# Cross-covariance attention and a gated feed-forward on one core: q and k loads queued 24 slots ahead, half of the batch-end products spread over the slots, and table loads placed ahead of PSUM copies

## The chip, the cores and the metric

The kernel runs on 1 core of one Trainium2 chip. The metric is device time in microseconds (us); 3 runs of the kernel before gave a median of 888.96 us (887.82 to 889.47). The engines are named as in the profile: PE is TensorE, DVE VectorE, ACT ScalarE, POOL GpSimd, and SP the engine that issues stores and transposes.

## The reference

For each of 4 batches, q, k and v are 6016 x 256. The columns of q and k are divided by their norms over the 6016 rows, a 256 x 256 score is made, a softmax is taken over its last axis, and v is multiplied by it. All 24064 rows then go through a gated feed-forward with 1536 hidden columns.

```python
qn = q / (np.linalg.norm(q, axis=1, keepdims=True) + 1e-06)
kn = k / (np.linalg.norm(k, axis=1, keepdims=True) + 1e-06)
s = kn.transpose(0, 2, 1) @ qn / tau
a = softmax(s)                      # over the last axis
x = (v @ a).reshape(B * S, D)
gate = 1.0 / (1.0 + np.exp(-(x @ w_gate)))
out = (gate * (x @ w_val)) @ w_out
```

## The kernel before

**The tiling.** A batch's 6016 rows are 47 tiles of 128 rows, in 12 chunks of 4 tiles (the last chunk has 3). The attention matrix is folded into the feed-forward's weights: G = a w_gate and H = a w_val (`gh`, 12 parts for each batch), so a chunk of v, transposed (`vT`), needs only two products: gate = vT G and val = vT H. The 1536 hidden columns are 12 slices of 128; one slice of one chunk is a *slot*, so a batch has 144 slots, and the main loop runs over b, ci (chunk) and f (slot).

**A slot.** `glu` (L460) puts two matmuls for `ps_gate` and two for `ps_val` on PE, a sigmoid on ACT (L481, to `g_sb`) and a multiplication on DVE (L482, to `hT`). `ps_gate` and `ps_val` have two buffers each, so PE can run two slots ahead of ACT and DVE. `a_sum` (L488, L499) makes sums of slices of `hT` on DVE, five for each half of a chunk: those of the first half in the chunk's own slots 6 to 10, those of the second half in slots 0 to 4 of the next chunk.

**The output products.** The product with w_out works on pairs of row tiles with seven products instead of eight, from such sums. A chunk of 4 tiles has 2 pairs, each of 42 matmuls into two PSUM banks (`ps_o`, 2 buffers): 84 in `out_work` (L530), done while the next chunk is in its slots. `run_work(work, share)` (L592) issues a share of what is left, normally 1 / (12 - f), so 7 products in each slot. When a bank is full, `evict` is put on a list; `flush` (L602) runs it: a copy on ACT from PSUM to `m_sb` (L564) and, after the second bank, `combine` (L515, five operations on POOL). `store` (L607) issues the chunk's output from SP at slot 4.

**The next batch's score.** During a batch, the score of the next one is made beside it. `side_work` (L703) hands out its steps by slot: `load_qk` (L124, two DMAs issued by POOL for a group of 4 tiles), `score` (matmuls into `ps_s`), squares on ACT and their accumulation on DVE, over slots 0 to 95. In batches 1 and 2 group g has its first score product in slot 8g, and its load 20 slots earlier, but not before slot 0: groups 0 to 2 are thus loaded in slot 0 itself, and the load of group 3 in slot 4 follows them on POOL. `qkpool` has 5 buffers for each of q and k. In batch 0 the loads stand 12 slots ahead. Each chunk also has a v load, for the chunk two further on, at its slot 0 (POOL, L139), and a transpose by DMA, for the next chunk, at its slot 2 (SP, L446).

**The batch end.** In chunks 9 and 10 of batches 0 to 2 (`block`) the slots hold no output products. All 84 stand in a block after slot 11, in four quarters; ahead of each quarter come the side steps of that place, and `flush` behind it. In chunk 9's block stand `wide_sqrt` (ACT) and two `wide_inv` (DVE); in chunk 10's `wide_scale` (DVE) and two `exps` (ACT). Square root, exponential and sigmoid need different tables on ACT: a table load stands where the function changes. Copies need none. The parts of G and H for the next batch are made in chunk 11.

**The end.** The last chunk's own output cannot lie beside another chunk: `end_rows` and `last_rows` multiply its 3 tiles plainly after its slots.

Of the kernel before, what the change touches and what calls it, by code (L numbers as in the profile page):

```python
# [11 lines left out]
ACT = mybir.ActivationFunctionType  # L12
# [33 lines left out]
def kernel(  # L46
# [20 lines left out]
    nc = tc.nc  # L67
# [5 lines left out]
    B, N, C = q.shape  # L73
# [4 lines left out]
    FC = DFF // P  # L78
    FG = 512
    NFG = DFF // FG  # L80
    TPC = 4
    CH = TPC * P
    NCH = (NT + TPC - 1) // TPC
    groups = [(t, min(TPC, NT - t)) for t in range(0, NT, TPC)]
# [58 lines left out]
    t0, nt = groups0[0]  # L143
# [289 lines left out]
    def gh(b, n, pl, tag, act=None):  # L433
        gh_store(b, n, gh_mms(b, n, pl, tag), n % 2 == 0 if act is None else act)
# [4 lines left out]
    def transpose_v(b, ci, ps=None, late=None):  # L439

        t0, nt = groups[ci]
        v_sb = vs.pop((b, ci))
        vT = vtpool.tile([P, TPC * CB, P], BF16, tag="vT", name="vT")
        flat = v_sb[:, :nt, :].rearrange("p t c -> p (t c)")
        if ps is None:
            nc.sync.dma_start_transpose(out=vT[:, : nt * CB, :], in_=flat)  # L446
        else:
            for n in range(nt * CB):
                nc.tensor.transpose(
                    out=ps[:, n, :], in_=flat[:, ds(n * P, P)], identity=ident_bf  # L450
                )
            half = nt * CB // 2 if late else nt * CB
            if late:
                late(vT[:, half : nt * CB, :], ps[:, half : nt * CB, :])
            nc.vector.tensor_copy(out=vT[:, :half, :], in_=ps[:, :half, :])
        vts[b, ci] = vT.rearrange("p (u cb) n -> p cb u n", cb=CB)
# [3 lines left out]
    def glu(b, ci, f, between=None):  # L460
        t0, nt = groups[ci]
        n = nt * P
        G, H = st[b]["gh"]
        vT = vts[b, ci]
        if f == 0:
            hts[b, ci] = hpool.tile([P, FC, CH], BF16, tag="hT", name="hT")
        ps_gate = psg.tile([P, CH], FP32, tag="g", name="ps_gate")
        ps_val = psv.tile([P, CH], FP32, tag="v", name="ps_val")
        for ps, w in ((ps_gate, G), (ps_val, H)):
            for ib in range(CB):  # L470
                mm(
                    ps[:, :n],
                    w[f // (FG // P)][:, ib, ds(f % (FG // P) * P, P)],
                    vT[:, ib, :nt, :],
                    start=(ib == 0),
                    stop=(ib == CB - 1),
                )
            if between is not None and w is G:
                between()
        g_sb = gpool.tile([P, CH], FP32, tag="g", name="g_sb")  # L480
        nc.scalar.activation(out=g_sb[:, :n], in_=ps_gate[:, :n], func=ACT.Sigmoid)  # L481
        nc.vector.tensor_tensor(  # L482
            out=hts[b, ci][:, f, :n], in0=ps_val[:, :n], in1=g_sb[:, :n], op=ALU.mult
        )
# [3 lines left out]
    def a_sum(b, ci, g, m):  # L488

        nt = groups[ci][1]  # L490
        half = nt // 2
        hT = hts[b, ci]
        if m == 0:
            sums[b, ci, g] = spool.tile(
                [P, len(A_SUMS), FC // 4, CH // 2], BF16, tag=f"s{g}", name="sums", bufs=2 - g
            )
        (r0, k0), op, (r1, k1) = A_SUMS[m]
        f0, f1 = g * (FC // 2), (g + 1) * (FC // 2)
        nc.vector.tensor_tensor(  # L499
            out=sums[b, ci, g][:, m, :, : half * P],  # L500
            in0=hT[:, f0 + k0 : f1 : 2, ds(r0 * half * P, half * P)],
            in1=hT[:, f0 + k1 : f1 : 2, ds(r1 * half * P, half * P)],
            op=op,
        )
# [84 lines left out]
                work.append((2, single, state, nt - 1, f))  # L589
        return work  # L590

    def run_work(work, share):  # L592

        left = sum(w[0] for w in work)
        upto = left * share
        done = 0
        while work and done < upto:
            cost, fn, *args = work.pop(0)
            fn(*args)
            done += cost  # L600

    def flush():  # L602
        while pending:
            fn, *args = pending.pop(0)
            fn(*args)

    def store():  # L607
        while stores:
            b, ci = stores.pop(0)
            t0, nt = groups[ci]  # L610
            nc.sync.dma_start(out=out_rows[b][:, t0 : t0 + nt, :], in_=ffn.pop((b, ci))[:, :nt, :])
# [37 lines left out]
    for g, (t0, nt) in enumerate(groups0):  # L649
# [6 lines left out]
        while adds:  # L656
            w, last_sq = adds.pop()
# [45 lines left out]
    def side_work(b):  # L703


        side = {}

        def at(slot, fn, *a):
            side.setdefault(divmod(slot, FC), []).append((fn, a))

        for ci in range(NCH):
            nb, nci = (b, ci + 1) if ci + 1 < NCH else (b + 1, 0)
            lb, lci = (b, ci + 2) if ci + 2 < NCH else (b + 1, ci + 2 - NCH)
            if (nb, nci) == (0, 1):
                at(8, lambda: transpose_v(0, 1, psm.tile([P, TPC * CB, P], BF16, tag="m", name="ps_tp")))
            elif nb < B:
                at(ci * FC + 2, transpose_v, nb, nci)
            if lb < B:
                at(ci * FC + 0, load_v, lb, lci)
            if (b, ci) == (0, 0):  # L720
                for i in range(FC // TPC):
                    at(i, load_w_out, i)
                    at(i + 2, sum_w_out, i)
        n = b + 1
        if n == B:
            return side
        first, last = (14 if b == 0 else 0), 8 * FC
        for g, (t0, nt) in enumerate(groups):
            s0 = first + g * (last - first) // NCH
            at(max(0, s0 - (12 if b == 0 else 20)), load_qk, n, t0, nt)  # L730
            for u in range(nt):
                at(first + (t0 + u) * (last - first) // NT, score, n, t0, u)
            if g == 0:
                at(s0, acc_start, n)
            for i, (fn, w) in enumerate(((acc_square, 0), (acc_add, 0), (acc_square, 1), (acc_add, 1))):
                at(s0 + 1 + 2 * i, fn, n, g, w)
        for i in range(6):
            at(8 * FC + 2 + i, acc_fold, n, *divmod(i, 3))
        at(9 * FC + 9, norms_mm, n)
        for ci, s, *call in (  # L740
            (9, 0, wide_sqrt, n),
            (9, 2, wide_inv, n, 0),
            (9, 3, wide_inv, n, 1),
            (10, 0, wide_scale, n),
            (10, 0, exps, n, 0),
            (10, 0, exps, n, 1),
        ):
            side.setdefault((ci, FC + s), []).append((call[0], call[1:]))
        at(11 * FC + 0, sums_both, n)
        at(11 * FC + 0, gh_tiles, n)  # L750
        for i in range(len(gh_order)):
            at(11 * FC + min(i + 1, FC - 1), gh, n, i, *((pss, "s"), (psm, "m"))[i % 2])
        return side
# [5 lines left out]
    prev = None  # L759
    for b in range(B):  # L760
        side = side_work(b)
        for ci in range(NCH):
            block = b + 1 < B and ci in (9, 10)
            for f in range(FC):
                first = (b, ci, f) == (0, 0, 0)
                glu(b, ci, f, (lambda: gh(0, 4, pso, "o", act=False)) if first else None)
                flush()
                if prev is not None:
                    if f == 4:
                        store()  # L770
                    if not block:
                        run_work(work, 1 / (FC - f))
                    if f < len(A_SUMS):
                        a_sum(*prev, 1, f)
                if f >= FC // 2 and f - FC // 2 < len(A_SUMS) and (b, ci) != (B - 1, NCH - 1):
                    a_sum(b, ci, 0, f - FC // 2)
                for fn, a in side.get((ci, f), ()):
                    fn(*a)
                if (b, ci) == (0, 0):
                    for i in gh_first.get(f, ()):  # L780
                        gh(0, i, pso, "o")
            if prev is not None and block:
                for s in range(TPC):
                    for fn, a in side.get((ci, FC + s), ()):
                        fn(*a)
                    run_work(work, 1 / (TPC - s))
                    flush()
            prev = (b, ci)
            if prev != (B - 1, NCH - 1):
                work = out_work(*prev)  # L790
# [40 lines left out]
```

## Time and profile before

| what | value |
|---|---|
| median of 3 runs | 888.96 us |
| the profiled execution | 889.01 us, of which the span from first to last instruction is 887.2 us |
| busy PE / DVE / ACT / POOL | 812.7 / 739.6 / 533.0 / 422.1 us |
| mean granted PE clock | 0.982 |
| DMA | 78.23 MB moved, 88 GB/s on average |

The busy times overlap, and the one nearest to the span is the candidate for what sets the end. A timeline row gives start, length, engine, line, operation, what is written and read, and in brackets how long the engine had been idle before and what ended the wait. Line 119 is the helper through which all matmuls go, so matmuls are told apart by their tiles. Rows of busy time by stage give the stage, its length, then busy time with the instruction count for PE, PE's weight loads, DVE, ACT and POOL, then the granted clock, the DMA engines' share and GB/s. A matmul's length is longer than the distance from one to the next, since they are pipelined; for throughput one takes the distance between starts.

### The profile page before, as it was taken

To read this page: it belongs to the slowest core of one execution; us is meant where nothing else is said; L and a number is where in the kernel's file an instruction comes from. 1 tells how busy PE (TensorE), PEld (TensorE's weight loads), DVE (VectorE), ACT (ScalarE), POOL (GpSimd) and SP (SyncE) were. 2 spreads that over 40 slices of the span, in tenths; PEclk is the share of its full clock that TensorE was granted. 3 is DMA by queue.
4 is the path that set the end of the run, shared out by engine and by line. 5 is a ranking of instruction groups with operands and counts; after the bars stand their busy time and mean duration, and the time that the engine had idled before them with its cause. 6 is when DMAs were issued, how large, how long until landed. Compare 5 with 4: busy or idle time off the path is not lost.

```text
span 887.2 us, 17830 instructions
## 1 busy us (share of the span) xinstructions
PE 812.7 (92%) x6772; PEld 501.3 (57%) x6772; DVE 739.6 (83%) x1236; ACT 533.0 (60%) x900; POOL 422.1 (48%) x623
## 2 busy tenths in 40 slices
PE   4899999999849999999984999999998999999997
PEld 2546666654525666665553566666555666666665
DVE  5698999998646999999864699999986898888885
ACT  3657666656635666665663566666566655555553
POOL 3655464534342465553434246555343345555554
PEclk9999999999988999999998899999999999999999
DMA  9975557322245565632234556563223223232311
GB/s 221 214 143 100 100 98 138 71 49 68 58 79 100 104 106 96 121 66 48 64 62 73 102 107 107 96 117 69 48 62 65 57 47 86 58 85 60 75 41 66
DMA packets 77926, 78.23 MB, mean 88 GB/s; under 512 B 50704, under 2 KB 55824, under 8 KB 77840
## 3 DMA queue, kind: packets, MB, share of 16 engines
q0 software_dynamic: 21216, 38.02, 25.9%
q1 hardware_dynamic: 56336, 38.48, 18.6%
q8 instruction: 53, 0.87, 0.4%
q10 hardware_dynamic: 288, 0.59, 0.2%
q14 instruction: 33, 0.27, 0.1%
HBM read 78.64 MB, written 24.64 MB: 116 GB/s over the span
## 4 chain that ended last, share of the span: by engine, by line
PE 71%; DVE 12%; DMA 6%; ACT 5%; issue 5%; POOL 1%; DVEq 0%; ACTq 0%; POOLq 0%
PE ps_gate L119 23%; PE ps_o L119 22%; PE ps_val L119 21%; DVE sums L499 6%; DVE hT L482 5%; DMA k_sb<-in_k_dram 5%; PE ps_s L119 3%; ACT g_sb L481 2%; PE ps_gh L119 2%; ACT sq L231 2%; DMA w_gate<-in_moe_w_gate_dram 1%; ACT m_sb L564 0%; ACT L304 0%; DVE acc L269 0%; DVE two L279 0%
## 5 line engine op out<-in xcount | busy, mean ns | idle before, releaser
L481 ACT ACTIVATE g_sb<-ps_gate 128x512 f32<-128x512 f32 (+1 forms) x576 | 338.3, 589 | 294.9 <-PE ps_gate L119 287.1
L482 DVE TENSOR_TENSOR hT<-ps_val,g_sb 128x512 bf16<-128x512 f32 (+1 forms) x576 | 387.0, 673 | 120.4 <-ACT g_sb L481 83.5
L119 PE MATMUL ps_val<-vT,gh_H 128*128 128x512 bf16 (+1 forms) x1152 | 339.2, 376 | 7.3 <-DVE hT L482 5.2
L119 PE MATMUL ps_gate<-vT,gh_G 128*128 128x512 bf16 (+1 forms) x1152 | 339.3, 376 | 2.2 <-ACT g_sb L481 2.2
L499 DVE TENSOR_TENSOR sums<-hT 128x768 bf16<-128x768 bf16 (+1 forms) x470 | 303.3, 645 | 0.0
L522 POOL TENSOR_TENSOR m_sb<-m_sb 128x256 f32<-128x256 f32 x91 | 65.8, 723 | 422.4 <-ACT m_sb L564 422.4
L119 PEld LDWEIGHTS <-sums 128*128 128x128 bf16 x2730 | 184.7, 98 | 98.7 <-DVE sums L499 21.3
L119 PEld LDWEIGHTS <-gh_H 128*128 128x128 bf16 x1152 | 112.9, 98 | 148.3 <-issue 24.5
L119 PE MATMUL ps_o<-w_sums,sums 128*128 128x128 bf16 x1638 | 152.5, 220 | 1.2 <-DVE sums L499 0.9
L119 PE MATMUL ps_o<-w_out_sb,sums 128*128 128x128 bf16 x1092 | 108.1, 219 | 12.2 <-DVE sums L499 12.2
L119 PEld LDWEIGHTS <-gh_G 128*128 128x128 bf16 x1152 | 99.6, 98 | 32.3 <-issue 3.1
L525 POOL TENSOR_TENSOR out_sb<-m_sb 128x128 f32<-128x128 f32 x182 | 112.6, 638 | 0.0
L119 PE MATMUL ps_s<-k_sb,q_sb 128*128 128x256 bf16 x376 | 73.4, 301 | 40.9 <-DMA k_sb<-in_k_dram 34.3
L119 PEld LDWEIGHTS <-hT 128*128 128x128 bf16 x1176 | 82.9, 98 | 47.4 <-issue 6.2
L564 ACT COPY m_sb<-ps_o 128x512 f32<-128x512 f32 (+1 forms) x182 | 95.6, 527 | 9.7 <-PE ps_o L119 9.6
L119 PE MATMUL ps_o<-w_sums,hT 128*128 128x128 bf16 x1092 | 90.1, 220 | 4.7 <-ACT m_sb L564 4.2
L523 POOL TENSOR_TENSOR m_sb<-m_sb 128x256 f32<-128x256 f32 x91 | 80.2, 881 | 7.1
L528 POOL TENSOR_TENSOR out_sb<-m_sb 128x256 f32<-128x256 f32 x91 | 78.5, 863 | 0.0
L119 PEld LDWEIGHTS <-q_sb 128*128 128x128 bf16 x376 | 34.3, 107 | 47.6 <-issue 36.5
L231 ACT ACTIVATE sq<-k_sb 128x1024 bf16<-128x1024 bf16 (+2 forms) x44 | 44.8, 1026 | 15.1 <-DMA k_sb<-in_k_dram 14.9
L269 DVE TENSOR_TENSOR acc<-acc,sq 128x1024 bf16<-128x1024 bf16 (+1 forms) x66 | 50.5, 766 | 0.0
L231 ACT ACTIVATE sq<-q_sb 128x1024 bf16<-128x1024 bf16 (+2 forms) x36 | 36.5, 1015 | 0.2 <-DVE acc L660 0.2
(79 smaller groups left out, 280.4 us busy)
## 6 DMA issues: line engine op xcount, KB each, us to landing
out_dram<-out_sb SPq DMA_DIRECT2D x44, 512.0 KB, 3.4
v_sb<-in_v_dram POOLq DMA_DIRECT2D x44, 256.0 KB, 5.2
q_sb<-in_q_dram POOLq DMA_DIRECT2D x35, 256.0 KB, 7.0
k_sb<-in_k_dram POOLq DMA_DIRECT2D x35, 256.0 KB, 7.8
q_sb<-in_q_dram POOLq DMA_DIRECT2D x4, 512.0 KB, 12.4
k_sb<-in_k_dram POOLq DMA_DIRECT2D x4, 512.0 KB, 14.8
w_f<-in_moe_w_out_dram SPq DMA_DIRECT2D x3, 512.0 KB, 15.4
out_dram<-out_sb SPq DMA_DIRECT2D x3, 384.0 KB, 6.7
```

Source lines behind the costliest of these rows:

```text
L119: nc.tensor.matmul(out, lhsT=lhsT, rhs=rhs, start=start, stop=stop, **kw)
L231: nc.scalar.activation(out=sq[:, :nt, :], in_=src[:, :nt, :], func=ACT.Square)
L269: nc.vector.tensor_tensor(out=acc[:, :nt, :], in0=acc[:, :nt, :], in1=st[b]["sq", w][:, :nt, :], op=ALU.add)
L481: nc.scalar.activation(out=g_sb[:, :n], in_=ps_gate[:, :n], func=ACT.Sigmoid)
L482: nc.vector.tensor_tensor(out=hts[b, ci][:, f, :n], in0=ps_val[:, :n], in1=g_sb[:, :n], op=ALU.mult)
L499: nc.vector.tensor_tensor(out=sums[b, ci, g][:, m, :, : half * P], in0=hT[:, f0 + k0 : f1 : 2, ds(r0 * half * P, half * P)], in1=hT[:, f0 ...
L522: nc.gpsimd.tensor_tensor(out=t, in0=t, in1=m[:, 3:4, :].to_broadcast([P, 2, P]), op=ALU.add)
L523: nc.gpsimd.tensor_tensor(out=t, in0=t, in1=m[:, 4:6, :], op=ALU.subtract)
L525: nc.gpsimd.tensor_tensor(out=blocks[:, mids, :], in0=m[:, 1 - n, :], in1=m[:, 4 + n, :], op=ALU.add)
L528: nc.gpsimd.tensor_tensor(out=ends, in0=t, in1=m[:, 0:2, :], op=ALU.add)
L564: nc.scalar.copy(m[:, n0:n1, :], state[bank][:, : (n1 - n0) * P].rearrange("p (n c) -> p n c", c=P))
```

## The change

Four things change, all of them places in the order; no instruction is added or dropped except that the table loads on ACT are asked for by name.

- *Loads.* In batches 1 and 2, group g is loaded 24 slots ahead of slot 8g. For groups 0 to 2 that place lies in the batch before, in slots 120, 128 and 136 (chunk 10, slots 0 and 8, and chunk 11, slot 4).
- *Products.* `run_work` takes `keep`, a number of products to leave. In chunks 9 and 10 the first pair's 42 products go into slots 0 to 10 and only the second pair's stand in the block, in two halves.
- *Tables.* In the blocks the load of the sigmoid's table is placed right behind the square root, and right behind the exponentials, and that of the exponential's table ahead of `wide_scale`. `flush` runs once before and once behind the block, so the copies come after the table loads.
- *The last chunk.* In the last chunk of the last batch the products of the chunk before are spread over 10 slots instead of 12, and `a_sum` stands ahead of `run_work` in all slots.

```diff
-    def run_work(work, share):
-
-        left = sum(w[0] for w in work)
-        upto = left * share
+    def run_work(work, share, keep=0):
+
+        upto = sum(w[0] for w in work[: len(work) - keep]) * share
         done = 0
-        while work and done < upto:
+        while len(work) > keep and done < upto:
...
-            at(max(0, s0 - (12 if b == 0 else 20)), load_qk, n, t0, nt)
+            if b == 0:
+                at(max(0, s0 - 12), load_qk, n, t0, nt)
+            elif s0 >= 24:
+                at(s0 - 24, load_qk, n, t0, nt)
...
+        if n + 1 < B:
+            for g, (t0, nt) in enumerate(groups[:3]):
+                at(NCH * FC - 24 + 8 * g, load_qk, n + 1, t0, nt)
...
+        table = nc.scalar.preload_act_table
         for ci, s, *call in (
             (9, 0, wide_sqrt, n),
-            (9, 2, wide_inv, n, 0),
-            (9, 3, wide_inv, n, 1),
+            (9, 0, table, ACT.Sigmoid),
+            (9, 1, wide_inv, n, 0),
+            (9, 2, wide_inv, n, 1),
+            (10, 0, table, ACT.Exp),
             (10, 0, wide_scale, n),
             (10, 0, exps, n, 0),
             (10, 0, exps, n, 1),
+            (10, 0, table, ACT.Sigmoid),
         ):
...
+            early = 1 if block else 2 if (b, ci) == (B - 1, NCH - 1) else 0
...
-                    if not block:
-                        run_work(work, 1 / (FC - f))
                     if f < len(A_SUMS):
                         a_sum(*prev, 1, f)
+                    held = len(work) if not block or f == 0 else held
+                    run_work(work, 1 / max(1, FC - early - f), held // 2 if block else 0)
...
             if prev is not None and block:
-                for s in range(TPC):
+                flush()
+                for s in range(3):
                     for fn, a in side.get((ci, FC + s), ()):
                         fn(*a)
-                    run_work(work, 1 / (TPC - s))
-                    flush()
+                    run_work(work, 1 / (2 - s) if s < 2 else 1)
+                flush()
```

How the change stands on ACT, in chunk 9 of batch 0 and its block. `g_sb` is a sigmoid, `m_sb` a copy of a bank, `n_sb` the square root. Before, from the chunk's second slot on:

```order
137 L481 ACTIVATE g_sb<-ps_gate 128x512 x11
138 L304 ACT_TABLE_LOAD
139 L304 ACTIVATE n_sb<-ps_n 128x258
140 L564 COPY m_sb<-ps_o 128x512
141 L564 COPY m_sb<-ps_o 128x384
142 L564 COPY m_sb<-ps_o 128x512
143 L564 COPY m_sb<-ps_o 128x384
144 L481 ACT_TABLE_LOAD
145 L481 ACTIVATE g_sb<-ps_gate 128x512 x12
```

The same place in the changed kernel:

```order
137 L481 ACTIVATE g_sb<-ps_gate 128x512 x6
138 L564 COPY m_sb<-ps_o 128x512
139 L481 ACTIVATE g_sb<-ps_gate 128x512 x5
140 L564 COPY m_sb<-ps_o 128x384
141 L304 ACT_TABLE_LOAD
142 L304 ACTIVATE n_sb<-ps_n 128x258
143 L796 ACT_TABLE_LOAD
144 L564 COPY m_sb<-ps_o 128x512
145 L564 COPY m_sb<-ps_o 128x384
146 L481 ACTIVATE g_sb<-ps_gate 128x512 x7
```

One copy of the first pair now lies among the sigmoids and one right behind the last of them; the sigmoid's table is loaded behind the square root, ahead of the two copies that are left, and no longer at the first sigmoid.

On POOL, from the v load in slot 0 of chunk 10 of batch 0 on, before (L139 loads v, L129 loads q or k, L522 to L528 are one `combine`):

```order
146 L139 DMA v_sb<-in_v_dram 128x1024
147 L522 TENSOR_TENSOR m_sb<-m_sb 128x2x128
148 L523 TENSOR_TENSOR m_sb<-m_sb 128x2x128
149 L525 TENSOR_TENSOR out_sb<-m_sb 128x128 x2
150 L528 TENSOR_TENSOR out_sb<-m_sb 128x2x128
```

In the changed kernel:

```order
146 L139 DMA v_sb<-in_v_dram 128x1024
147 L129 DMA q_sb<-in_q_dram 128x1024
148 L129 DMA k_sb<-in_k_dram 128x1024
149 L129 DMA q_sb<-in_q_dram 128x1024
150 L129 DMA k_sb<-in_k_dram 128x1024
151 L522 TENSOR_TENSOR m_sb<-m_sb 128x2x128
152 L523 TENSOR_TENSOR m_sb<-m_sb 128x2x128
153 L525 TENSOR_TENSOR out_sb<-m_sb 128x128 x2
```

The q and k loads of groups 0 and 1 of batch 2's score now stand between the v load and the next `combine`, two groups one behind the other.

## Prediction

> **What bounds the kernel now.** First the page's busy shares, then who TensorE (PE) waited for, then busy time by stage, then the timeline at the places that stood out.
>
> ```profile
> PE 812.7 (92%) x6772; PEld 501.3 (57%) x6772; DVE 739.6 (83%) x1236; ACT 533.0 (60%) x900; POOL 422.1 (48%) x623
> PE ps_s L119 <- DMA k_sb<-in_k_dram: 34.3, 7, 12.5
> ```
>
> PE is the busiest engine and VectorE (DVE) the next. Of PE's waits one stands out: the score product `ps_s` waits for a load of k, 34.3 us in 7 waits, the longest 12.5 us. The stages show where (each row: stage, its length, then busy time of PE, weight loads, DVE, ACT, POOL, then the granted clock, DMA share, GB/s):
>
> ```profile
> 254.10:266.58 12.48, 0.01 (x1) 0.03 (x1) 1.26 (x2) 0.24 (x1) 7.71 (x14) 0.65 0.66 126
> 266.58:271.60 5.02, 5.02 (x22) 2.66 (x23) 1.23 (x3) 2.14 (x3) 0.00 (x0) 0.50 1.13 205
> 271.60:283.40 11.80, 11.80 (x87) 7.19 (x85) 9.31 (x17) 7.89 (x13) 3.48 (x5) 1.00 0.25 47
> 270.00:436.00 166.00, 161.31 (x1356) 100.13 (x1355) 153.41 (x250) 107.51 (x181) 78.23 (x112) 1.00 0.47 87
> 488.95 0.58 PE L119 MATMUL ps_s<-k_sb,q_sb 128*128 128x256 bf16 x2 [12.34 <-DMA k_sb<-in_k_dram]
> ```
>
> In the first slot of batch 1 PE stands for 12.48 us, then works 5.02 us at half the clock, and is full again from 271.60. Batch 2 begins the same way (12.34 us before 488.95). Everywhere else in a batch PE is busy 97% of the time at clock 1.00 (161.31 of 166.00), so it sets the pace and DVE (92%) is close behind. The other holes lie at the end of each of batches 0 to 2, in chunks 9 and 10, where a chunk's 12 slots are followed by a block of products:
>
> ```profile
> 197.18:209.20 12.02, 11.49 (x57) 4.94 (x55) 11.83 (x23) 7.09 (x13) 4.37 (x6) 1.00 0.33 75
> 209.20:214.12 4.92, 4.86 (x86) 4.73 (x84) 4.43 (x7) 3.56 (x6) 1.72 (x3) 1.00 0.04 9
> 214.12:227.24 13.12, 11.78 (x52) 4.63 (x50) 10.50 (x20) 8.67 (x14) 4.99 (x9) 1.00 0.37 81
> 227.24:233.47 6.23, 4.84 (x85) 4.72 (x84) 2.43 (x5) 3.78 (x7) 1.84 (x4) 1.00 0.01 3
> 233.47:252.75 19.28, 18.46 (x164) 11.80 (x162) 14.40 (x29) 11.98 (x23) 7.95 (x14) 1.00 0.25 55
> ```
>
> Rows one and three are the slots of chunks 9 and 10, two and four their blocks, five is chunk 11. In the slots of chunk 9 DVE is busy 11.83 of 12.02 us: it, not PE, sets the pace there.
>
> **Part one, the loads.** In batches 1 and 2 the q and k loads of groups 0 to 3 all stand in the first slots:
>
> ```profile
> 257.39 0.57 POOL L139 DMA_DIRECT2D v_sb<-in_v_dram  x1
> 258.48 0.55 POOL L129 DMA_DIRECT2D k_sb<-in_k_dram  x1
> k_sb<-in_k_dram POOLq DMA_DIRECT2D x4, 256.0 KB, 7.6
> ```
>
> The first k load is issued at 258.48 and its user runs at 266.58, 8 us later; the last row, of the stage from 300 to 345 us, gives 7.6 us to landing. The change issues group 0 at slot 120 of the batch before, in chunk 10, some 30 us ahead of its use by the stage rows (13.12 + 6.23 + 19.28 less what the queue is late), so landing is covered several times over. What is late next is nothing on PE: from 271.60 it never waits. Gain for batch 1: 12.48 of standing plus half of 5.02, since that work at clock 1.00 takes 2.51, so 15.0. For batch 2: 12.34, and 2.3 for a slow stretch a little shorter, so 14.6. Together 29.6.
>
> The rule on the slow stretch differs a little: the Trainium skill (TensorE: Matmul & The Clock Gate, Part 1: The HAM clock gate) has the array back at full rate after about 3.4 us of sustained work; that would make each slow stretch cost 1.7 and the term 28.2. Here the row shows 5.02 us at 0.50.
>
> POOL issues the same number of loads, each of about 0.55 us as above, so its own time does not grow. The moved ones pass `combine` of chunks 9 and 10 in POOL's order, and stand behind the v load of chunk 10. There lies a cost: the transpose that makes `vT` of chunk 11 then runs beside four q and k loads.
>
> ```profile
> 218.62 0.57 POOL L139 DMA_DIRECT2D v_sb<-in_v_dram  x1
> 223.78 1.24 SPq L446 DMA_TRANSPOSE vT<-v_sb  x1
> vT<-v_sb SPq DMA_TRANSPOSE x3, 4.4
> vT<-v_sb SPq DMA_TRANSPOSE x1, 12.3
> ```
>
> It is issued 5.2 us after the v load. It took 4.4 us to land beside two loads (300 to 345 us) and 12.3 beside eight (256 to 268 us). Beside four I take 7, nearer to the first. Issued near 223.5 as now, it lands at 230.5. By the walk below, chunk 11's first gate must be done near 232.0, so `vT` must be there by 231.3: no cost, and 4.5 us each in batches 0 and 1 if 12.3 held.
>
> By the Trainium skill (DMA: Bandwidth & Descriptors, Queues, rings and completion order) each DMA engine takes turns between its queues packet by packet, so a transpose would never wait for all that is queued on POOL's; by that the loss is nothing. The row of 12.3 speaks against it, so I keep the loss as a rival.
>
> **Part two, the products of one pair.** A slot of `glu` alone takes PE 0.86 us, and 84 products in a row 4.92, so 0.0585 each and 2.46 for the 42 that move:
>
> ```profile
> 198.04 0.59 PE L119 MATMUL ps_gate<-vT,gh_G 128*128 128x512 bf16 x2
> 198.90 0.59 PE L119 MATMUL ps_gate<-vT,gh_G 128*128 128x512 bf16 x2
> ```
>
> Twelve slots are 10.32. Chunk 9's slots last 12.02; I leave 0.3 of the rest to the six short matmuls of `norms_mm`, so PE has 1.4 free and the last sigmoid comes 1.06 later. Chunk 10's last 13.12 with 2.8 free: the products fit, DVE sets the pace as before.
>
> **Part three, the order on ACT.** Chunk 9's block, before:
>
> ```profile
> 208.95 0.60 ACT L481 ACTIVATE g_sb<-ps_gate 128x512 f32<-128x512 f32 x1 [0.27 <-PE ps_gate L119]
> 209.57 1.28 ACT L304 ACT_TABLE_LOAD   x1
> 210.86 0.39 ACT L304 ACTIVATE n_sb<-ps_n 128x258 f32<-128x258 f32 x1
> 214.81 1.28 ACT L481 ACT_TABLE_LOAD   x1
> 216.11 1.09 ACT L481 ACTIVATE g_sb<-ps_gate 128x512 f32<-128x512 f32 x2
> 213.16 0.95 DVE L310 RECIPROCAL n_sb<-n_sb 128x128 f32<-128x128 f32 x1
> 216.74 0.69 DVE L482 TENSOR_TENSOR hT<-ps_val,g_sb 128x512 bf16<-128x512 f32 x1 [2.62 <-ACT g_sb L481]
> 232.72 0.59 ACT L564 COPY m_sb<-ps_o 128x512 f32<-128x512 f32 x1 [1.26 <-PE ps_o L119]
> 233.67 0.48 ACT L564 COPY m_sb<-ps_o 128x384 f32<-128x384 f32 x1 [0.36 <-PE ps_o L119]
> ```
>
> From the sigmoid's end (209.55) to the next sigmoid pass 6.56 us: table load, square root, four copies that wait for the products, table load. The change leaves one late copy 0.48, load 1.28, root 0.39, load 1.28, and two copies 0.59 + 0.48 (lengths from chunk 10's rows): 4.50. With the start at 210.61, the next sigmoid begins at 215.1 and DVE's `hT` 0.63 after it as now, at 215.7 instead of 216.74. DVE's inversion (root's end to 214.11, 2.86) ends at 215.6, so it does not come later. Gain 1.0, and DVE carries it through chunk 10. Its block:
>
> ```profile
> 226.80 0.60 ACT L481 ACTIVATE g_sb<-ps_gate 128x512 f32<-128x512 f32 x1 [0.41 <-PE ps_gate L119]
> 229.70 0.91 ACT L378 ACTIVATE e_sb<-x_sb,shift 128x256 bf16<-128x256 f32 x2 [1.01 <-DVE x_sb L320]
> 234.17 1.28 ACT L481 ACT_TABLE_LOAD   x1
> 235.46 0.87 ACT L481 ACTIVATE g_sb<-ps_gate 128x384 f32<-128x384 f32 x2
> 231.13 0.83 PE L119 MATMUL ps_o<-w_sums,hT 128*128 128x128 bf16 x12 [1.39 <-ACT m_sb L564]
> 235.99 0.56 DVE L482 TENSOR_TENSOR hT<-ps_val,g_sb 128x384 bf16<-128x384 f32 x1 [6.32 <-ACT g_sb L481]
> ```
>
> From 227.40 to 235.46 are 8.06 us. After: the exponentials still start 2.30 in (they wait for DVE; the late copy and the load end at 1.76), last 0.91, then load 1.28, copies 1.07: 5.56. Gain 2.5. PE's wait of 1.39 for buffers goes, but PE then waits for that sigmoid. Chunk 11 follows from there unchanged. Per batch 3.5, three times 10.5. Bounds: 2.0 where the fuller slots of chunks 9 and 10 couple PE and DVE tighter than the walk has it; 5.2 where PE, now with 10.32 + 2.46 + 2.46 = 15.2 per chunk against 16.94 and 19.35 taken, has almost no wait left (5.8, less 0.6).
>
> **Part four, the last chunk** packs its products into 10 slots, so each sum is wanted earlier.
>
> ```profile
> 869.65 0.23 PE L119 MATMUL ps_o<-w_out_sb,sums 128*128 128x128 bf16 x1 [0.54 <-DVE sums L499]
> 869.98 0.61 DVE L499 TENSOR_TENSOR sums<-hT 128x768 bf16<-128x768 bf16 x1
> 871.24 0.55 DVE L499 TENSOR_TENSOR sums<-hT 128x768 bf16<-128x768 bf16 x1
> 872.02 0.49 PE L119 MATMUL ps_gate<-vT,gh_G 128*128 128x384 bf16 x2
> ```
>
> Already PE waits 0.54 here. Products 33 and 39 of a pair, counted from 0, are the first to need the second group's fourth and fifth sums; at 8.4 products a slot they stand in slots 3 and 4, at 7 in slots 4 and 5. So PE waits for the fourth sum until 870.6 (869.98 + 0.61), and only then issues slot 4's gate, whose sigmoid, `hT` and fifth sum follow in a row: about 0.5 each for four steps of this width, 872.6. After the last four products of that row it has done 5 slots and 43 products at 872.9; now it has done 6 slots and 42 products at 872.02. A 384-wide slot is three quarters of 0.86, or 0.65: a loss of 1.5. The earlier copies and store win nothing, since the last rows' stores end the run. Bounds: 0 to 1.8.
>
> **Sum.** 29.6 + 10.5 - 1.5 = 38.6 off the profiled execution's 889.01 us, which is 0.05 over the median: 850.4.
>
> **Rivals.** (a) *The blocks give nothing*: slots lengthen by all that the blocks lose. For it: DVE is at 11.83 of 12.02. Against: PE's free 1.4 and 2.8 us, and DVE's idle 2.62 and 6.32, which the products do not cause. Time 889.0 - 29.6 + 1.5 = 860.9. (b) *The transpose becomes the wait*: 12.3 to landing, twice 4.5: 859.4. For it the one row; against it that half as many loads stand there. (c) *The loads do not come early*, because POOL reaches them late and half of each stall stays: 865. Against: POOL is 48% busy. (d) *Slower*: a load waits on POOL for the buffer of the group five earlier, and `combine` and the v load behind it hold PE. The group's last reader stands near slot 8g - 32, the load at 8g - 24; eight slots of about 1.25 us (11.80 us hold some nine) are 10 us of slack. It decides from 38.6 / 18 = 2.1 us of PE standing at each of the 18 loads, and at 2.2 gives 890; the reader would have to be over 12 us late, and no wait of PE or ACT in the quoted stages is near that but the stall itself.
>
> **How the numbers follow.** Forecast 0.80, (a) 0.09, (b) 0.06, (c) 0.03, (d) 0.02. The forecast's own ends: 889.0 - 30.0 - 15.6 = 843.4 at the bounds that gain most, and, if only the standing time comes back (24.8) and the blocks and the last chunk go at their worst, 889.0 - 24.8 - 6.0 + 1.8 = 860.0. Range 844 to 861: it takes in (a) and (b). A measurement of this kernel can tell 0.2%, 1.8 us. Faster 0.97, same 0.01 (the far end of (c)), slower 0.02.
>
> **What would show it.** Right: no `ps_s` wait over 1 us after 50 us; granted clock 1.00 at both batch starts; from chunk 9's last sigmoid to the next near 4.5 us, from chunk 10's near 5.6; DVE's idle there near 0 and 4; PE's waits for `sums` in the last chunk up by about 1.5. Wrong: a `vT` wait at chunk 11, slots of chunks 9 and 10 over 13.4 us, or a clock under 1.00 in the long stretches.

## The result, and the profile after

| | before | after |
|---|---|---|
| median | 888.67 us (887.82 to 889.47, 4 runs) | 850.32 us (849.52 to 850.74, 4 runs) |
| the profiled execution | 889.01 us, span 887.2 | 849.52 us, span 847.7 |
| mean granted clock | 0.982 | 0.992 |

The ratio is 0.9567 (95% interval 0.9551 to 0.9584): faster, by 38.4 us between the medians, where 38.6 was forecast.

To see where the time left, the trace is divided into chunks: a chunk lasts from the start of its first `hT` multiplication on DVE (L482) to the start of the next chunk's. In us:

| chunk | before, batches 0, 1, 2 | after, batches 0, 1, 2 | gained |
|---|---|---|---|
| 0 | (start-up), 31.00, 30.62 | (start-up), 15.92, 15.92 | 15.08 + 14.70 |
| 1 to 8 | 16.37 to 18.09 | the same within 0.02 | 0 |
| 9 | 18.30, 18.31, 18.30 | 17.01, 17.01, 17.01 | 3.88 |
| 10 | 19.25, 19.24, 19.25 | 16.87, 16.87, 16.88 | 7.12 |
| 11 | 18.02, 18.01, 18.01 | 18.05, 18.28, 18.05 | -0.34 |
| last chunk of batch 3, to the end | 21.34 | 23.08 | -1.73 |

The loads give 29.78, the blocks 10.66 with chunk 11's share, the last chunk takes 1.73. Some 0.8 more lies in the first 60 us, where nothing was moved and where chunk 0 of batch 0 took 14.26 to 14.85 in the kernels below, the one before 14.76. Together 39.5, the difference of the spans (887.2 less 847.7).

The same in the views. First the page's busy shares, then PE's waits over the whole run (what it waited for: us in total, times, longest):

```profile
PE 798.8 (94%) x6760; PEld 499.0 (59%) x6772; DVE 741.2 (87%) x1236; ACT 531.7 (63%) x900; POOL 424.7 (50%) x623
```

```profile
PE ps_o L119 <- DVE sums L499: 13.1, 28, 1.1
PE ps_s L119 <- DMA k_sb<-in_k_dram: 10.6, 5, 3.3
PE ps_o L119 <- ACT m_sb L564: 8.3, 6, 1.7
```

Before, the third of these rows was

```profile
PE ps_o L119 <- ACT m_sb L564: 4.2, 3, 1.4
```

The waits for k fell from 34.3 us in 7 to 10.6 in 5; from 50 us on there is none. But PE's waits for copies out of PSUM (`m_sb`) have risen: 8.3 us in six waits, two at each of three batch ends, where there was one. PE's share of the span rose from 92 to 94% and DVE's from 83 to 87%: the same work in a shorter span.

The stages at the start of batch 1 (length; busy PE, weight loads, DVE, ACT, POOL; granted clock, DMA share, GB/s):

```profile
248.31:249.51 1.20, 1.20 (x11) 0.72 (x10) 0.75 (x1) 1.02 (x3) 0.00 (x0) 1.00 0.00 0
249.51:265.50 15.99, 15.90 (x121) 9.76 (x119) 13.71 (x24) 11.18 (x20) 9.75 (x16) 1.00 0.57 101
252.00:420.00 168.00, 162.88 (x1389) 101.85 (x1387) 155.65 (x254) 110.92 (x186) 84.75 (x123) 1.00 0.49 90
```

The score product stands at 249.51, the seam between the first two rows, and there is neither a hole nor a slow stretch: PE is busy 15.90 of 15.99 us of chunk 0 at clock 1.00. The third row, of nearly a whole batch, has the 97% that it had.

Now ACT at the ends of chunk 9's and chunk 10's slots (time, length, engine, line, operation; in brackets the wait just before):

```profile
209.17 0.60 ACT L481 ACTIVATE g_sb<-ps_gate 128x512 f32<-128x512 f32 x1 [0.43 <-PE ps_gate L119]
209.67 0.47 ACT L564 COPY m_sb<-ps_o 128x384 f32<-128x384 f32 x1
210.16 1.28 ACT L304 ACT_TABLE_LOAD   x1
211.45 0.39 ACT L304 ACTIVATE n_sb<-ps_n 128x258 f32<-128x258 f32 x1
211.86 1.28 ACT L796 ACT_TABLE_LOAD   x1
213.15 0.97 ACT L564 COPY m_sb<-ps_o 128x512 f32<-128x512 f32 x2
214.00 1.23 ACT L481 ACTIVATE g_sb<-ps_gate 128x512 f32<-128x512 f32 x2
...
225.63 0.60 ACT L481 ACTIVATE g_sb<-ps_gate 128x512 f32<-128x512 f32 x1 [0.43 <-PE ps_gate L119]
226.62 1.28 ACT L796 ACT_TABLE_LOAD   x1
227.91 0.91 ACT L378 ACTIVATE e_sb<-x_sb,shift 128x256 bf16<-128x256 f32 x2
228.84 1.28 ACT L796 ACT_TABLE_LOAD   x1
230.13 0.97 ACT L564 COPY m_sb<-ps_o 128x512 f32<-128x512 f32 x2
230.98 0.51 ACT L481 ACTIVATE g_sb<-ps_gate 128x384 f32<-128x384 f32 x1
```

From the end of one sigmoid to the start of the next are now 4.23 us in chunk 9 (209.77 to 214.00; before 6.56) and 4.75 in chunk 10 (226.23 to 230.98; before 8.06). Each time two copies stand behind the second table load. PE shows what that does to it, and so does the last chunk:

```profile
213.79 0.38 PE L119 MATMUL ps_o<-w_sums,hT 128*128 128x128 bf16 x4 [1.01 <-ACT m_sb L564]
230.77 0.55 PE L119 MATMUL ps_o<-w_sums,hT 128*128 128x128 bf16 x7 [1.75 <-ACT m_sb L564]
829.10 0.51 PE L119 MATMUL ps_o<-w_out_sb,sums 128*128 128x128 bf16 x6 [0.67 <-DVE sums L499]
830.03 0.34 PE L119 MATMUL ps_o<-w_out_sb,sums 128*128 128x128 bf16 x3 [0.43 <-DVE sums L499]
832.34 0.34 PE L119 MATMUL ps_o<-w_sums,sums 128*128 128x128 bf16 x3 [1.15 <-DVE sums L499]
```

The first two are products that stand in the following chunk's first slot and want a PSUM buffer which the late copy still holds. The last three belong to the last chunk: there PE's waits for `sums` are 2.6 us in four waits, where before they were 0.5 in one.

DVE's first multiplication behind each block, and between them the last one of chunk 10:

```profile
214.65 0.69 DVE L482 TENSOR_TENSOR hT<-ps_val,g_sb 128x512 bf16<-128x512 f32 x1 [0.32 <-ACT g_sb L481]
226.34 0.68 DVE L482 TENSOR_TENSOR hT<-ps_val,g_sb 128x512 bf16<-128x512 f32 x1
231.53 0.56 DVE L482 TENSOR_TENSOR hT<-ps_val,g_sb 128x384 bf16<-128x384 f32 x1 [3.72 <-ACT g_sb L481]
```

DVE's idle time there was 2.62 and 6.32 and is now 0.32 and 3.72. Last, the transposed v of chunk 11, which now runs beside four q and k loads:

```profile
vT<-v_sb SPq DMA_TRANSPOSE x1, 7.6
```

It lands in 7.6 us, where it took 3.0 before with no load of q or k beside it, and no wait of PE for `vT` appears.

### The profile page after: what moved, and what is told of

The parts are those of the page before. It is cut to its first block, busy times and chain, and to the rows that moved or that the text cites. A ratio compares the mean times of both kernels' runs of the same rounds, so it can differ in the third digit from the quotient of the medians.

```text
span 847.7 us, 17813 instructions
## 1 busy us (share of the span) xinstructions
PE 798.8 (94%) x6760; PEld 499.0 (59%) x6772; DVE 741.2 (87%) x1236; ACT 531.7 (63%) x900; POOL 424.7 (50%) x623
## 4 chain that ended last, share of the span: by engine, by line
PE 73%; DVE 8%; ACT 7%; DMA 6%; issue 4%; POOL 2%; POOLq 0%; ACTq 0%; DVEq 0%
PE ps_gate L119 24%; PE ps_val L119 23%; PE ps_o L119 21%; DMA k_sb<-in_k_dram 6%; DVE sums L499 4%; DVE hT L482 4%; PE ps_s L119 3%; ACT g_sb L481 2%; PE ps_gh L119 2%; ACT sq L231 2%; ACT m_sb L564 1%; ACT L796 1%; POOL out_sb L525 0%; POOL m_sb L523 0%; DVE acc L269 0%
## 5 line engine op out<-in xcount | busy, mean ns | idle before, releaser
L482 DVE TENSOR_TENSOR hT<-ps_val,g_sb 128x512 bf16<-128x512 f32 (+1 forms) x576 | 387.7, 674 | 78.1 <-ACT g_sb L481 71.0
L522 POOL TENSOR_TENSOR m_sb<-m_sb 128x256 f32<-128x256 f32 x91 | 65.9, 724 | 383.4 <-ACT m_sb L564 383.4
L119 PEld LDWEIGHTS <-sums 128*128 128x128 bf16 x2730 | 187.9, 98 | 109.0 <-DVE sums L499 21.2
L119 PE MATMUL ps_o<-w_sums,sums 128*128 128x128 bf16 x1638 | 154.4, 219 | 1.9 <-DVE sums L499 1.7
L119 PE MATMUL ps_o<-w_out_sb,sums 128*128 128x128 bf16 x1092 | 109.9, 219 | 11.6 <-DVE sums L499 11.4
L525 POOL TENSOR_TENSOR out_sb<-m_sb 128x128 f32<-128x128 f32 x182 | 114.8, 650 | 0.0
L119 PEld LDWEIGHTS <-gh_G 128*128 128x128 bf16 x1152 | 96.8, 98 | 14.5 <-DVE gh_G L431 0.4
L119 PE MATMUL ps_s<-k_sb,q_sb 128*128 128x256 bf16 x376 | 71.8, 295 | 17.9 <-DMA k_sb<-in_k_dram 10.6
L528 POOL TENSOR_TENSOR out_sb<-m_sb 128x256 f32<-128x256 f32 x91 | 77.7, 853 | 0.0
```

What stands on the lines that cost most here:

```text
L119: nc.tensor.matmul(out, lhsT=lhsT, rhs=rhs, start=start, stop=stop, **kw)
L482: nc.vector.tensor_tensor(out=hts[b, ci][:, f, :n], in0=ps_val[:, :n], in1=g_sb[:, :n], op=ALU.mult)
L522: nc.gpsimd.tensor_tensor(out=t, in0=t, in1=m[:, 3:4, :].to_broadcast([P, 2, P]), op=ALU.add)
L525: nc.gpsimd.tensor_tensor(out=blocks[:, mids, :], in0=m[:, 1 - n, :], in1=m[:, 4 + n, :], op=ALU.add)
L528: nc.gpsimd.tensor_tensor(out=ends, in0=t, in1=m[:, 0:2, :], op=ALU.add)
```

## The experiments

Eight kernels tell the parts apart. The theory is the prediction's walk, and that its terms add. The rivals: the parts need each other; the order of the tables, not the moved products, makes the blocks' gain (or does harm); any lead of the loads would do; and the slow stretch is not due to the standing. The kernel before had a median of 888.12 us (7 runs) beside the first four kernels and 888.79 us (11 runs) beside the others; beside the changed kernel it was 888.67. So differences of medians across these groups are uncertain by some 0.7 us.

**The loads alone.** The kernel before with the loads' part of the change and nothing else:

```diff
-            at(max(0, s0 - (12 if b == 0 else 20)), load_qk, n, t0, nt)
+            if b == 0:
+                at(max(0, s0 - 12), load_qk, n, t0, nt)
+            elif s0 >= 24:
+                at(s0 - 24, load_qk, n, t0, nt)
...
+        if n + 1 < B:
+            for g, (t0, nt) in enumerate(groups[:3]):
+                at(NCH * FC - 24 + 8 * g, load_qk, n + 1, t0, nt)
```

> The kernel before with only the q and k loads moved 24 slots ahead; blocks, tables and the last chunk as before. Theory A (the terms of the sum are independent, and the load term is the standing time plus the slow-clock stretch at the two batch starts): the first chunk of batches 1 and 2 takes about 15.9 us instead of 31.0 and 30.6, all other chunks as before, the time is 888.7 - 29.8 = 858.9 us. Theory B (a transfer that is no longer hidden takes part of it back: the transpose for chunk 11 stands beside four more loads): its landing is over 11 us instead of about 7.6, a wait of PE for the transposed v shows at chunk 11, and the time is 861 to 868 us.

Measured 859.14 us (858.62 to 859.32), ratio 0.9674 (0.9657 to 0.969): 29.0 off. Chunk 0 takes 15.92 us in both batches, as in the changed kernel, while chunks 9 and 10 keep 18.30 and 19.23. The transposed v of chunk 11 beside its four loads:

```profile
vT<-v_sb SPq DMA_TRANSPOSE x1, 6.9
```

The load term needs nothing of the other parts, and no wait for `vT` comes with it.

**The blocks alone.** The change without its loads and with the last chunk over 12 slots as before:

```diff
-            early = 1 if block else 2 if (b, ci) == (B - 1, NCH - 1) else 0
+            early = 1 if block else 0
```

(and the load lines of the diff above taken back)

> The kernel before with only the blocks of chunks 9 and 10 changed (one pair's products into the slots, tables ahead of copies); loads and the last chunk as before. Theory A (independent terms): chunks 9 and 10 take 17.0 and 16.9 us instead of 18.3 and 19.2 in each of batches 0 to 2, the first chunks of batches 1 and 2 stay at about 31, the time is 888.7 - 10.7 = 878.0 us. Theory B (what the blocks give shows only while the loads are early, since the batch start would wait for the same loads anyway): the stall at the batch starts grows by what the blocks give, and the time stays within 886 to 889 us.

Measured 878.4 us (876.66 to 879.33), ratio 0.989 (0.9871 to 0.9909): 9.7 off. Chunks 9 and 10 take 17.01 and 16.87, exactly as in the changed kernel, chunk 0 of batches 1 and 2 takes 31.39 and 30.73, or 0.39 and 0.11 more than before. So the blocks' gain does not fall into the stall behind it. Loads alone and blocks alone give 38.7, less the 1.3 of the next run 37.4, against 38.4 for all: the terms add to within 1.0 us, and chunk by chunk the lengths are those of the changed kernel.

**The last chunk over 12 slots.** The changed kernel with the line of `early` above and nothing else.

> The changed kernel with the products in the last chunk of the last batch spread over 12 slots again. Theory A (packing them into 10 slots makes PE wait for sums on DVE and gains nothing at the end): PE's waits for sums in the last chunk fall from 2.6 to about 0.5 us, the time is 1.5 to 2.0 us less, 848.6 us. Theory B (the earlier copies and the earlier store let the end come sooner, and the waits only take the place of others): the time is 0 to 2 us more, 850.3 to 852.3 us.

Measured 849.02 us (848.66 to 849.32), ratio 0.9561 (0.9547 to 0.9575): 1.3 less than the changed kernel. In the window from 820 us to the end PE's waits are

```profile
PE ps_o L119 <- DVE sums L499: 0.5, 1, 0.5
```

as before the change, and the last chunk takes 21.34 again instead of 23.08. Packing the last products into 10 slots costs 1.3 us by the medians, a little under what was expected, and 1.73 by the traces, and it is the wait for the sums. The medians alone would not carry this: the intervals of the two ratios overlap.

**Copies ahead of the table loads.** The changed kernel without its three entries for tables. The copies then come first, and the sigmoid's table is loaded at the first sigmoid:

```diff
             (9, 0, wide_sqrt, n),
-            (9, 0, table, ACT.Sigmoid),
...
-            (10, 0, table, ACT.Exp),
...
-            (10, 0, table, ACT.Sigmoid),
```

> The changed kernel without the table loads asked for by name, so that in the blocks the two copies from PSUM come ahead of the sigmoid's table load and the load stands at the first sigmoid. Theory A (ACT's chain from the last sigmoid of the block to the next holds the same operations in either order, 4.5 and 5.6 us, so moving the table gives nothing; with the copies first PE no longer waits 1.0 and 1.7 us for the PSUM buffers): the times between those sigmoids change by less than 0.3 us, PE's waits for the copies fall from 8.3 to under 2 us in all, the time is 0.5 to 4 us less, near 848 us. Theory B (the table load ahead of the copies is what hides it, as the products are still running then): each of the six blocks loses up to one load of 1.28 us, the time is 853 to 858 us.

Measured 848.08 us (847.84 to 848.28), ratio 0.9551 (0.9536 to 0.9565): 2.2 us faster than the changed kernel by the medians. ACT at both blocks:

```profile
209.41 0.60 ACT L481 ACTIVATE g_sb<-ps_gate 128x512 f32<-128x512 f32 x1 [0.43 <-PE ps_gate L119]
...
211.97 0.96 ACT L564 COPY m_sb<-ps_o 128x512 f32<-128x512 f32 x2
212.95 1.28 ACT L481 ACT_TABLE_LOAD   x1
214.24 1.09 ACT L481 ACTIVATE g_sb<-ps_gate 128x512 f32<-128x512 f32 x2
...
225.66 0.60 ACT L481 ACTIVATE g_sb<-ps_gate 128x512 f32<-128x512 f32 x1 [0.43 <-PE ps_gate L119]
...
228.76 0.94 ACT L564 COPY m_sb<-ps_o 128x512 f32<-128x512 f32 x2
229.72 1.28 ACT L481 ACT_TABLE_LOAD   x1
231.01 0.87 ACT L481 ACTIVATE g_sb<-ps_gate 128x384 f32<-128x384 f32 x2
```

and PE's waits for the copies over the whole run:

```profile
PE ps_o L119 <- ACT m_sb L564: 1.0, 3, 0.3
```

From the end of one sigmoid to the start of the next it is the same 4.23 and 4.75 us (210.01 to 214.24, 226.26 to 231.01): two copies and a table load take the same time in either order. But ahead of the load the copies free their PSUM buffers 1.28 us sooner, and PE's waits for them fall from 8.3 to 1.0 us. Chunk 10 then takes 16.65 and chunk 11 17.71 in all three batches, against 16.87 and 18.05 to 18.28; chunks 9 to 11 give 1.9 us together. The tables' part of the change, put like this, brings nothing and costs some 2 us.

**The tables alone.** To see whether the early tables do anything for the full blocks of 84 products, the kernel of the first experiment with the three entries added:

```diff
+            (9, 0, table, ACT.Sigmoid),
...
+            (10, 0, table, ACT.Exp),
...
+            (10, 0, table, ACT.Sigmoid),
```

> The kernel before with the loads moved (as in the run with the loads alone, 859.1 us) and the table loads placed as in the change, while all 84 products stay in the block in four quarters. Theory A (a table load placed earlier on ACT only changes places with copies, and here it delays the copies that free the PSUM buffers for the block's later products): chunks 9 and 10 keep 18.3 and 19.2 us within 0.4 each, the time is 858 to 859.5 us. Theory B (the table load fills ACT's idle time in the block, 1.1 to 1.3 us twice): each block gains up to 1.2 us, the time is 852 to 856 us.

Measured 861.05 us (860.9 to 862.27), ratio 0.969 (0.9677 to 0.9704): 1.9 us slower than without them by the medians, 1.4 by the ratios, whose intervals overlap, and outside what either side expected. ACT and PE in chunk 10's block of batch 0, and the stage behind PE's wait:

```profile
230.18 1.28 ACT L795 ACT_TABLE_LOAD   x1
231.47 0.97 ACT L564 COPY m_sb<-ps_o 128x512 f32<-128x512 f32 x2
```

```profile
232.11 1.44 PE L119 MATMUL ps_o<-w_sums,hT 128*128 128x128 bf16 x12 [2.82 <-ACT m_sb L564]
```

```profile
232.11:235.50 3.39, 3.39 (x34) 3.39 (x34) 0.00 (x0) 0.91 (x2) 2.90 (x5) 0.53 0.15 32
```

With all products in the block, a buffer that is wanted in its middle waits behind the table load: PE stands for 2.82 us, and then its clock falls to 0.53 for a stage of 3.39 us. Chunk 10 takes 20.66, 19.15 and 20.55 us in the three batches. The wait is 2.82 in all three; in the 3.39 us behind it the clock is 0.53, 1.00 and 0.56. Where the clock stayed up, chunk 10 is no longer than without the tables (19.24), so what they cost here is mainly the slow stretch behind the wait. The traced execution is the slowest of the four, with a mean clock of 0.988; the other three, at 0.992, took 1.1 to 1.4 us less, and how often their clock fell is not shown. In none of the three batches do the tables shorten a full block by more than 0.1 us. So the gain of the blocks is not the tables' order: it needs the products out of the way. With the products came two smaller moves, the flush around the block and `wide_inv` one place earlier; no run takes these apart from the products.

**Matmuls in the stall.** The kernel before with 48 matmuls whose result nobody reads (0.22 us each) at the start of batches 1 and 2, so that PE works while the k load is out:

```diff
+                if b in (1, 2) and (ci, f) == (0, 0):
+                    busy(48)
```

> The kernel before with 48 matmuls of 128x512 that nobody reads put ahead of the first score product of batches 1 and 2, where PE stands 12.5 and 12.3 us; at about 0.22 us each they end some 2 us before the load lands. Nothing of the output changes. Theory A (half of the 5 us at clock 0.50 behind the stall is lost to the clock, and the standing itself is 12.4): the stretch behind the load runs at clock 1.00, the first chunks take 2.3 to 2.6 us less, 28.5 and 28.2 us, the time is 883.5 us. Theory B (the slow stretch costs nothing, as ACT and DVE would hold PE there anyway): the first chunks stay at 31.0 and 30.6 us, the time is 888 us.

The extra matmuls, the score product behind them, and the stages from there on:

```profile
253.91 10.52 PE L119 MATMUL ps_busy<-ones_wide,ones_bf 128*128 128x512 bf16 x48
266.64 0.38 PE L119 MATMUL ps_s<-k_sb,q_sb 128*128 128x256 bf16 x2 [2.21 <-DMA k_sb<-in_k_dram]
```

```profile
264.40:266.64 2.24, 0.03 (x1) 0.03 (x1) 0.00 (x0) 0.00 (x0) 0.00 (x0) 1.00 1.11 203
266.64:271.90 5.26, 5.26 (x45) 3.33 (x46) 2.87 (x6) 3.22 (x6) 0.00 (x0) 1.00 1.18 203
```

The load lands when it did, at 266.64 against 266.58, but now the work behind it runs at clock 1.00: 45 matmuls in 5.26 us, where it was 22 in 5.02. Chunk 0 takes 28.65 and 28.16, or 2.35 and 2.46 less, about half of the slow stretch. That is what the prediction took for it, and in this execution it shows the slow stretch to be a consequence of PE's idling. The traced execution took 884.16 us, 4.6 under the kernel before; the median of six was 886.06 (884.16 to 887.99), ratio 0.9969 (0.9958 to 0.998), only 2.7 under it and 2.6 over the 883.5 that theory A expected. What the other executions lost is not shown by a trace; their mean clock, 0.987 to 0.995, was above the 0.976 to 0.982 of the kernel before. It stays open.

**Loads 8 slots ahead.** The changed kernel with a lead of 8 slots in place of 24:

```diff
-            elif s0 >= 24:
-                at(s0 - 24, load_qk, n, t0, nt)
+            elif s0 >= 8:
+                at(s0 - 8, load_qk, n, t0, nt)
...
-            for g, (t0, nt) in enumerate(groups[:3]):
-                at(NCH * FC - 24 + 8 * g, load_qk, n + 1, t0, nt)
+            for g, (t0, nt) in enumerate(groups[:1]):
+                at(NCH * FC - 8 + 8 * g, load_qk, n + 1, t0, nt)
```

> The changed kernel with the loads of batches 2 and 3 queued 8 slots ahead instead of 24, still across the batch boundary. A slot is about 1.3 us there, so the lead is some 10.5 us, and a k load lands 7.8 us after its issue. Theory A (a lead over the landing time covers it): no wait of PE for these loads, 850 us. Theory B (POOL reaches a load 3 to 5 us late, since it stands behind combine and the v load, so the lead has to cover that too): PE waits for k loads at the groups that stand behind the v load, 1 to 4 us each, the time is 860 to 885 us.

Measured 860.8 us (859.88 to 861.23), ratio 0.9683 (0.967 to 0.9696): 10.5 us over the changed kernel. PE, POOL and the stages at the start of batch 1:

```profile
263.13 0.38 PE L119 MATMUL ps_s<-k_sb,q_sb 128*128 128x256 bf16 x2 [2.16 <-DMA k_sb<-in_k_dram]
```

```profile
250.95 0.73 POOL L522 TENSOR_TENSOR m_sb<-m_sb 128x256 f32<-128x256 f32 x1 [6.06 <-ACT m_sb L564]
...
254.62 0.55 POOL L129 DMA_DIRECT2D q_sb<-in_q_dram  x1
255.14 0.56 POOL L129 DMA_DIRECT2D k_sb<-in_k_dram  x1
```

```profile
261.00:263.13 2.13, 0.00 (x1) 0.10 (x1) 1.43 (x2) 0.21 (x1) 1.76 (x3) 1.00 1.13 159
263.13:264.80 1.67, 1.67 (x10) 0.98 (x9) 0.20 (x1) 0.82 (x2) 1.67 (x4) 0.84 0.19 41
264.80:267.40 2.60, 2.60 (x10) 1.22 (x9) 1.54 (x3) 1.32 (x2) 2.37 (x5) 0.50 0.57 76
267.40:272.00 4.60, 4.60 (x35) 2.68 (x34) 3.60 (x8) 2.76 (x5) 0.00 (x0) 0.97 1.12 208
```

This is group 1's first product, in slot 8 of chunk 0; its load stands in slot 0 of the same chunk. The product was due at 260.97 (263.13 less the wait), and the batch's first score product, in slot 0, started at 250.47, so a load issued at its place would go out near 250.5. POOL was then idle, but waiting for ACT's copies (6.06 us, to 250.95); the load stands behind `combine` and the v load and goes out at 255.14, some 4.7 us late and 8.0 us ahead of the product's start. That is theory B's 3 to 5 us. Chunk 0 takes 19.45 and 19.33 us (15.92 with the long lead) and chunk 2 takes 18.57 and 18.23 (16.91). PE stands twice per batch, for 2.16 and 1.54 us in batch 1 and for 2.04 and 1.20 in batch 2, and in batch 1 the clock then shows 0.50 over a stage of 2.60 us. A lead that covers a load of some 8 us on paper is not enough: the load has to be reached in POOL's order first.

**Both mends.** The changed kernel with copies ahead of the table loads and the last chunk over 12 slots (both edits above together).

> The changed kernel without the named table loads (copies first) and with the last chunk's products over 12 slots: the two gains found so far together. Theory A (they lie at different places and add): chunks 10 and 11 at 16.7 and 17.7 us, PE's waits for sums in the last chunk 0.5 us, the time is 848.1 - 1.5 = 846.5 us. Theory B (one takes the place of the other): 848 us.

Measured 846.35 us (846.01 to 846.66, 5 runs), ratio 0.9523 (0.951 to 0.9536): 4.0 us faster than the change, the fastest of all. Against the kernel before the gain is 42.4 us, with 38.4 of it the change's own. Chunks 10 and 11 take 16.65 and 17.71 in all three batches, the last chunk 21.35. Alone the two mends were worth 1.3 and 2.2 by the medians, together 4.0; by the chunks they add, 1.9 and 1.73.

## Why the prediction was right

**The loads: 29.6 forecast, 29.78 in the chunks.** Both halves of the term were seen apart. The standing time is the first experiment's, and the half of the slow stretch is that of the matmuls in the stall (2.35 and 2.46 against the 2.5 and 2.3 taken). Landing was covered as forecast; the run with 8 slots shows that the cover was needed and that a shorter one fails, by POOL's lateness, which is the mechanism of rival (c) in a kernel where it does hold. The transposed v was put at 7 us beside four loads and landed in 6.9 and 7.6, so rival (b), at 12.3, did not come. Rival (d), slower, needed waits at POOL's loads of 2.1 us each; there is no wait for k at all after 50 us.

**The slow stretch.** The row had 5.02 us at clock 0.50. By the Trainium skill (TensorE: Matmul & The Clock Gate, Part 1: The HAM clock gate), with about 3.4 us, the term would have been 28.2; the chunks give 29.78, and the measured stretch was the better guide. The other side of the same rule, that the clock falls after an idle window of about 3.4 us, is not borne out as a threshold by the runs: it fell after waits of 2.04, 2.16 and 2.82 us, all under it.

**The blocks: 10.5 forecast, 10.66 in the chunks.** Chunk 9 was to win 1.0 a batch and won 1.29: its last sigmoid came 1.02 later, where 1.06 was taken, and its path from sigmoid to sigmoid took 4.23, not 4.50, mainly since the two copies behind the load took 0.85 (213.15 to 214.00) and not 1.07.

Chunk 10 was to win 2.5 and won 2.38. "The products fit, DVE sets the pace as before" held: from its first `hT` to the last sigmoid DVE has no idle time, in 10.06 us before (216.74 to 226.80) and in 10.98 now (214.65 to 225.63). These two lengths hold different amounts of DVE's work, so they say nothing of the pace. The last `hT` does. Before it stood here:

```profile
228.21 0.68 DVE L482 TENSOR_TENSOR hT<-ps_val,g_sb 128x512 bf16<-128x512 f32 x1
```

From the first `hT` to the last were 11.47 us (216.74 to 228.21) and are 11.69 (214.65 to 226.34). With the copies first, and the same products in the slots, they are 11.50, so of the 0.22 only 0.03 is rival (a). The exponentials start 1.57 behind the last `hT` instead of 1.49. From their start to the next sigmoid are 3.07 us (227.91 to 230.98); they were 5.76 (229.70 to 235.46), and the walk had 3.26, the copies again taken too long. That gives 2.69, less 0.22 and 0.08, which is the 2.38 to within 0.01. The path from sigmoid to sigmoid fell further, from 8.06 to 4.75 where 5.56 was forecast, because the last sigmoid now lies later beside DVE's chain: the last `hT` starts 0.71 behind it, before 1.41. That part of the path is no gain.

The step that failed is "PE's wait of 1.39 for buffers goes, but PE then waits for that sigmoid. Chunk 11 follows from there unchanged". The wait did not go: PE waits for the copies, 1.01 and 1.75 us, because the change put them behind the table load, and chunk 11 is 0.03 to 0.27 longer. The walk had the copies as a length on ACT, not as what frees a buffer for PE. The run with the copies first prices that at 2.2 us by the medians; there chunk 11 is 0.3 shorter than before. So the 10.66 lies so near 10.5 partly by luck: over three batches chunk 9 gave 0.9 more than forecast, chunks 10 and 11 together 0.7 less.

**The last chunk: -1.5 forecast, -1.73 in the trace.** The waits for `sums` rose from 0.5 to 2.6 us. Counted along PE's rows, 1.58 of it stands at products 33 and 39 of the first pair (0.43 at 830.03, 1.15 at 832.34), the places named; 1.03 stands at two earlier sums (0.36 at 826.27, 0.67 at 829.10), which the walk did not have. The run that undoes it gives back 1.3 by the medians and 1.73 in its trace.

**The signs that were to show it.** No wait for k after 50 us, clock 1.00 at the batch starts, DVE's idle 0.32 and 3.72 (near 0 and 4): right. From sigmoid to sigmoid it is 4.23 and 4.75 (near 4.5 and 5.6 were listed), and the waits for `sums` rose by 2.1 and not 1.5. One sign against the forecast did come up: counted as in the prediction's rows, from a chunk's first gate to the block's first product, chunk 9's slots take 13.02 us (196.38 to 209.40) but chunk 10's 14.11 (211.75 to 225.86), over the 13.4 it had set. The time came as forecast all the same, since PE now starts the chunk further ahead of DVE's first `hT` and DVE ends it less far behind PE. The sign watched PE's slots, while DVE set the pace. What the list lacked is PE's wait for the copies.

## What to carry to other kernels

A stall on a load costs its standing time and the half-clock work behind it, and a lead cures both only if it also covers the time until the issuing engine gets to the load in its order: 24 slots did, 8 did not, for a load that took 8.0 us to land. When a row of operations on an engine is reordered, look at what each of them releases, not only at when the row ends: a table load ahead of two copies left the row as long as it was and cost some 2 us. And run the parts one at a time even when the total comes out as forecast, since the right sum here held errors that cancelled and two harmful parts worth 4.0 us.

## What the runs showed of the hardware

- The granted clock can fall after short waits. In the run with 8 slots it was 0.50 over a stage of 2.60 us that began 1.67 behind a wait of 2.16, and 0.53 over the 3.64 us behind one of 2.04. In the run with the tables alone the same wait of 2.82 us was followed by 0.53, 1.00 and 0.56 in the three batches. It stayed at 1.00 after a wait of 2.21 (with matmuls ahead of it) and after those of 1.75. The length of the wait alone does not decide it; what else does was not tried.
- A transpose by DMA takes longer the more loads stand beside it. That of chunk 11 took 3.0 us with no load of q or k beside it, and 6.9 and 7.6 with four, the first in the run that moves the loads alone. At a batch start it took 12.3 beside eight; beside two, in the kernel before, 3.2 to 5.3.
